# Local attention, then a two-matrix MLP: where the second batch's keys and queries are loaded and turned

## The chip, the cores and the metric

The kernel runs on one core of one Trainium2 chip. The metric is the device time of one execution in microseconds, the median of several runs; less is better. Engines are named as in the profile: PE (TensorE), PEld (its weight loads), DVE (VectorE), ACT (ScalarE), POOL (GpSimd) and SP (SyncE, here only an issuer of DMAs).

## The reference

Batch B = 8, heads H = 8, sequence S = 576, head width D = 64, 8 global positions. Cut to what matters:

```python
mask = np.abs(pos[:, None] - pos[None, :]) <= 32 | is_global[:, None] | is_global[None, :]
scores = np.where(mask, (q @ k.T) / 8, -1e9)
attn = softmax(scores)                       # with 1e-9 added to the sum
x = (attn @ v).transpose(0, 2, 1, 3).reshape(4608, 512)
h = x @ w_in                                 # 512 x 2048
g = h + sin(alpha * h) ** 2 / (alpha + 1e-9)
out = g @ w_out                              # 2048 x 512, float32
```

All inputs are float32 in HBM. The kernel computes in bfloat16, so every load from HBM through POOL's queue is a cast as well.

## The kernel before

The order of the work is written out by hand. For each batch b there are three pieces: `attention(b)`, `gemm1(b)` (x times w_in, and the snake function) and `gemm2(b)` (times w_out). Attention of batch b + 1 and gemm2 of batch b run interleaved on PE: `fill(n)` puts n matrix products of gemm2 between pieces of attention. The program therefore reads attention(0), gemm1(0), attention(1) with gemm2(0), gemm1(1), attention(2) with gemm2(1), and so on.

**gemm1.** It works through 16 blocks `nt` of 128 columns of w_in. For a block PE makes 8 matrix products (`chunks`, L1161) into one of three PSUM buffers (zn, zr, zd in turn); ACT takes the sine into `sb` (L1194); the square goes to ACT (L1197) or to DVE (L1199), as the table `ON_ACT_FIRST` says; DVE multiplies and adds into row nt of `H2` (L1200), which frees the PSUM buffer for block nt + 3.

**The first batches.** Keys and queries have to reach SBUF with the head width on the partitions. Batch 0's are loaded lying (tokens on the partitions) into rows 2 to 7 of H2 and turned by PE. Batches 2 and later are cast to DRAM by POOL (`cast_qk`: kd, qd) and turned by transposing DMAs on SP (`turn_qk`: kt, qt), then copied into place on DVE (`place`, L369). Batch 1's are also loaded lying: `load_lying` (L713) issues four loads into the upper halves of KD and VD, which attention(0) uses until its end, `turn_lying` (L729) turns a third of them on PE with 96 small products into the two PSUM buffers zo, and `place_lying` copies them out: keys on DVE (L737) into KX, queries on ACT (L743) into QX. The three thirds are turned behind blocks 7, 9 and 11 of gemm1(0); the keys are copied ahead of blocks 8, 10 and 12, the queries ahead of blocks 9, 11 and 13. zo is also used by `turn_kq` at block 4, which turns the global keys and queries (L769).

**V.** Batch 0's V is loaded by 16 small DMAs into VD. For batch 1 and later `cast_v` (L343) casts V to DRAM on POOL's queue (vd), and `load_v` (L418) loads it on SP's queue in four DMAs into VX (VD for even batches); `load_vg` (L422) adds the global rows, from VGb, which POOL casts (L761) from what `gather(v, gv)` brought. The numerators of attention (L1009, into zn) read VX; the first of them stand behind the third pair of heads' first scores.

**The queues.** All DMAs that cast are issued by POOL, in program order, on one queue: w_in in four quarters (L430), w_out in four quarters (L436), lying loads, vd, kd, qd. SP's queue has the gathers, the stores of the results (L1261, from osb), the logarithms kept for a later check (LC, L815), VX, MASKT and the transposes.

Of the kernel before, what the change touches and what calls it, by code (L numbers as in the profile page):

```python
# [12 lines left out]
DT = mybir.dt  # L13
# [5 lines left out]
NG = 8  # L19
KT = 48  # L20
# [229 lines left out]
def kernel(  # L250
# [11 lines left out]
    nc = tc.nc  # L262
    B, H, S, D = q.shape
# [3 lines left out]
    NT12 = S // KT  # L267
    NT6 = NT12 // 2
    NK = KT + NG
    NHP = H // 2  # L270
# [121 lines left out]
    def load_v0(hps):  # L392
        for hp in hps:
            for t in range(2):
                for y in range(2):
                    r = t * D + y * 24
                    nc.gpsimd.dma_start(
                        out=VD[r : r + 24, hp, :, t * D : t * D + D],
                        in_=v[0, 2 * hp + t].rearrange("(i a y) d -> y a i d", a=24, y=2)[y],
                    )  # L400

    def load_vg0():
        for h in range(H):
            t = h % 2
            nc.sync.dma_start(
                out=VD[t * D + KT : t * D + NK, h // 2, :, t * D : t * D + D],
                in_=VG0[h::H][:, None, :].to_broadcast([NG, NT12, D]),
            )
# [18 lines left out]
    def load_w_in(gs):  # L427
        for g in gs:
            cols = slice(g * DFF // 4, (g + 1) * DFF // 4)
            nc.gpsimd.dma_start(  # L430
                out=w_in[:, :, cols], in_=moe_w_in[:, cols].rearrange("(c p) n -> p c n", p=P)
            )

    def load_w_out():
# [11 lines left out]
    HK = HH * NT12  # L446
    nat = {w: H2[0 : D + HK, 2 + 3 * w : 5 + 3 * w, :].rearrange("p n c -> p (n c)")[:, 0 : KT * D] for w in (0, 1)}
    gq, gk, gv = [
        H2[0 : NG * B, nt, 0 : 2 * H * D].bitcast(DT.float32).rearrange("p (h d) -> p h d", d=D)
        for nt in (13, 14, 15)  # L450
    ]

    banks = mctx.enter_context(tc.tile_pool(name="banks", bufs=1, space=PSUM))
    zn, zd = [banks.tile([P, 2, 512], DT.float32, name=name) for name in ("zn", "zd")]
# [127 lines left out]
    load_v0((1, 2))  # L582
    load_w_in((1,))
    load_v0((3,))
    load_w_in((2, 3))
    load_vg0()
    gather(q, gq)

# [115 lines left out]
    for e, c0 in ((0, 20), (1, 16)):  # L704
        own = M2[:, :, e].rearrange("p t (x c) -> p t x c", x=2)[:, :, :, c0 : c0 + 24]
        nc.vector.tensor_tensor(out=own, in0=own, in1=farv[:, :, e], op=ALU.max)

    lie = [t[:, NHP * NT12 * D :] for t in (kflat, vflat)]

    def load_lying(t):  # L710

        for w, src in ((1, k), (0, q)):
            nc.gpsimd.dma_start(  # L713
                out=lie[t][D * w : D * w + NHP * NT12],
                in_=src[1].rearrange("(hp t) (i r) d -> t hp i (r d)", t=2, r=KT)[t],
            )

    R16 = KT // 3
    lain = [z.bitcast(DT.bfloat16)[:, 0 : R16 * NHP * NT12] for z in (zo[0][:], zo[1][:])]
# [14 lines left out]
    def place_lying(w, third, copy):  # L734
        A = slice(third * R16 // 2, (third + 1) * R16 // 2)
        if w == 1:
            copy(  # L737
                out=KX[1][:, :, :, 0:KT].rearrange("p h i (y a) -> p h i y a", y=2)[:, :, :, :, A],
                in_=lain[1].rearrange("p (a y h i) -> p h i y a", y=2, h=NHP, i=NT12),
            )  # L740
            return
        for y in range(2):
            copy(  # L743
                out=QX[1][:, :, y, PAD : PAD + 6 * SEG].rearrange("p h (m c) -> p h m c", c=SEG)[
                    :, :, :, 4:
                ].rearrange("p h m (e a) -> p h m e a", e=2)[:, :, :, :, A],
                in_=lain[0].rearrange("p (a y h m e) -> p y h m e a", y=2, h=NHP, m=6, e=2)[:, y],
            )
# [388 lines left out]


    ON_ACT = (1, 3, 5, 7, 9, 11, 13)
    ON_ACT_FIRST = (1, 3, 5, 7, 8, 10, 12, 14)  # L1140
    ON_ACT_SECOND = (1, 3, 5, 7, 9, 10, 12, 13)

    def gemm1(b):


        while len(waiting) > 1:
            fill(1)
        xT = xTs[b]
        r0 = (b % 2) * S
        more = b == B - 1  # L1150
        W = SG if more else S
        hr = tc.alloc_tile_pool(name="hr", bufs=1, space=PSUM)
        hs = {}

        def chunks(nt, cs, parts=slice(0, 2)):
            if nt not in hs:
                hs[nt] = (zn, None, zd)[nt % 3] or hr.tile([P, 2, 512], DT.float32, name="zr")
            h = hs[nt]
            for c in cs:
                for h_part, lo, hi in halves(h, W)[parts]:  # L1160
                    nc.tensor.matmul(  # L1161
                        out=h_part, lhsT=w_in[:, c, nt * P : (nt + 1) * P], rhs=xT[:, c, lo:hi],
                        start=(c == 0), stop=(c == CT - 1), skip_group_check=True,
                    )

        on_act = (ON_ACT_FIRST, ON_ACT_SECOND, ON_ACT)[min(b, 2)]
        for nt in range(NT):
            if b == 1 and nt in (10, 12):
                for which, t, y in PLACES[nt - 6 : nt - 4]:
                    place(2, which, t, y, nc.vector.tensor_copy)  # L1170
            if b == 0 and 8 <= nt < 14:
                third, late = divmod(nt - 8, 2)
                place_lying(1 - late, third, nc.scalar.copy if late else nc.vector.tensor_copy)
            if b == 0 and nt == 4:
                turn_kq()
            if b == 0 and nt == 10:

                cast_globals_v()
                for part in range(3):
                    place_globals(1, part, nc.gpsimd.tensor_copy)  # L1180
                load_vg(1)
            if nt == 0:

                for n in range(2):
                    chunks(n, range(CT - 1), slice(0, 2 - more))
                for n in range(2 * more):
                    chunks(n, range(CT - 1), slice(1, 2))
            chunks(nt, range(CT - 1, CT) if nt < 2 else range(CT))
            h = columns(hs[nt], W)
            fill((GROUP_LAST if more else PER_GROUP)[nt])  # L1190
            if b == 0 and nt in (7, 9, 11):
                turn_lying((nt - 7) // 2)
            sb = spool.tile([P, SG], DT.bfloat16, name="sb")
            nc.scalar.activation(out=sb[:, 0:W], in_=h, func=AF.Sin, scale=alphaT[:, nt : nt + 1])  # L1194
            s2 = spool.tile([P, SG], DT.bfloat16, name="s2")
            if nt in on_act:
                nc.scalar.activation(out=s2[:, 0:W], in_=sb[:, 0:W], func=AF.Square)  # L1197
            else:
                nc.vector.tensor_tensor(out=s2[:, 0:W], in0=sb[:, 0:W], in1=sb[:, 0:W], op=ALU.mult)  # L1199
            nc.vector.scalar_tensor_tensor(  # L1200
                out=H2[:, nt, r0 : r0 + W], in0=s2[:, 0:W], scalar=recipT[:, nt : nt + 1], in1=h,
                op0=ALU.mult, op1=ALU.add,
            )
        hr.release()
# [103 lines left out]
    def phase_a(b_att, b_moe):  # L1308
        def beside(at):

            if b_moe is None:
                if at == 0:
                    second_half()
                    gather(v, gv)
                if at == NHP - 1:
                    load_lying(0)
                if at == NHP:
                    load_lying(1)
                    cast_v(1)
                    for half in range(2):  # L1320
                        rows = slice(half * D, (half + 1) * D)
                        nc.sync.dma_start(out=MASKT[rows], in_=MASK[rows, half * NT6 : (half + 1) * NT6])
                    load_w_out()
                    load_v(1)
                return
            if at == 2 and b_att == B - 1:
                global_rows(slice(0, B - 1))
            if b_att == 5 and at == 3:
                load_columns()
            if 0 <= at < 2:  # L1330
                square_x(b_moe, at)
            if at == 2 and 1 < b_att and b_att + 2 < B:
                pace(xTs[b_att][0:1, 0, 0:1])
                cast_qk(b_att + 2)
                cast_v(b_att + 2)
            if b_moe == 0 and at == 1:
                turn_qk(2)
            for which, t, y in places_at(b_att, at):
                place(b_att + 1, which, t, y, nc.vector.tensor_copy)

        if b_moe is not None:
            waiting.append(gemm2(b_moe))
        attention(b_att, beside)

    phase_a(0, None)
    for b in range(B):
        if b == 1:
            pace(turned[2][0][0:1, 0:1])
            cast_v(2)
            cast_qk(3)  # L1350
            cast_v(3)
        if 0 < b < B - 1:
            load_v(b + 1)
            load_vg(b + 1)
        if b == B - 1:
            global_rows(slice(b, B))
        gemm1(b)
        if b + 1 < B:
            if b == 0:
                cast_qk(2)  # L1360
            elif b + 2 < B:
                turn_qk(b + 2)
            phase_a(b + 1, b)
# [50 lines left out]
```

## Time and profile before

| what | value |
|---|---|
| median of 3 runs (lowest to highest) | 361.01 us (360.44 to 361.14) |
| the profiled execution, its own time | 360.89 us |
| its span, first to last instruction | 359.1 us |
| mean granted TensorE clock | 0.992 |
| PE busy | 325.6 us (91%) |
| ACT busy | 286.4 us (80%) |
| DVE busy | 274.8 us (77%) |
| POOL busy | 58.9 us (16%) |
| DMA bytes, POOL's queue (q0) and SP's (q1) | 18.52 MB and 22.98 MB |

Busy time is the sum over an engine's instructions in one profiled execution; a line of the timeline gives the start, the duration, the engine and line, what is written and read, and in brackets how long the engine stood idle before and which event ended that. The rows of a DMA issue show when the engine issued it, not when its data landed; "DMA to landing" counts from the start of the issue to the last byte's arrival. In the rows of a stretch, PEclk is the share of TensorE's full clock that was granted, and GB/s what all DMA queues moved.

### The profile page before, as it was taken

Reading aid. Unit: us, or ns where it says so; the run is one execution under the profiler, and the core shown is the slowest. Engines: PE = TensorE matmul, PEld = TensorE weight load, DVE = VectorE, ACT = ScalarE, POOL = GpSimd, SP = SyncE. Lnnn points to the kernel's source line nnn. Section 1 sums busy time; section 2 is a strip of 40 time slices with the busy share of each in tenths; the row PEclk is TensorE's granted clock in tenths of the full one; section 3 lists DMA queues with packets and bytes.
Section 4 is the critical chain, followed back from the end, with each engine's and each line's share of the span. In section 5 each row is a group of like instructions: output and inputs, shape, how many; then the busy total and the mean of one; then the engine's idle time right before and its main releaser. Section 6 shows DMA issues by size and latency. Waiting matters only on the chain.

```text
span 359.1 us, 10959 instructions
## 1 busy us (share of the span) xinstructions
PE 325.6 (91%) x4484; PEld 206.8 (58%) x4484; DVE 274.8 (77%) x536; ACT 286.4 (80%) x428; POOL 58.9 (16%) x85
## 2 busy tenths in 40 slices
PE   2668888999899999999999999899999998999992
PEld 1557655556555765577557655576567655664552
DVE  6876866887979787978798788878887876788620
ACT  7779768987889898988998889688988887887510
POOL 7965410051004000400040004000000000004200
PEclk9999989999999999999999999999999999999998
DMA  7999999669988936695759754993251021002132
GB/s 111 114 142 158 160 222 239 143 107 206 189 147 163 171 71 153 126 187 100 133 112 185 146 103 90 197 144 84 63 112 42 2 62 35 29 0 58 51 87 67
DMA packets 87764, 42.27 MB, mean 118 GB/s; under 512 B 72378, under 2 KB 82362, under 8 KB 87322
## 3 DMA queue, kind: packets, MB, share of 16 engines
q0 software_dynamic: 44944, 18.52, 43.1%
q1 hardware_dynamic: 42762, 22.98, 29.1%
q8 instruction: 37, 0.61, 0.7%
q14 instruction: 21, 0.17, 0.2%
HBM read 41.97 MB, written 20.77 MB: 175 GB/s over the span
## 4 chain that ended last, share of the span: by engine, by line
PE 57%; ACT 14%; DVE 13%; DMA 7%; issue 5%; POOL 2%; DVEq 0%; ACTq 0%; POOLq 0%
PE zo L1247 25%; PE zn L1161 9%; DVE H L1200 6%; PE zr L1161 6%; PE zd L1161 5%; ACT sb L1194 5%; PE ring L971 3%; DMA VD<-in_q_dram 3%; DMA H<-in_q_dram 3%; PE zd L1009 2%; DVE s L1199 2%; ACT L947 2%; ACT E L980 2%; ACT s L1197 2%; PE zn L1009 2%
## 5 line engine op out<-in xcount | busy, mean ns | idle before, releaser
L1247 PE MATMUL zo<-w_out,H 128*128 128x512 bf16 (+1 forms) x576 | 148.8, 377 | 0.2 <-DVE E L981 0.2
L1161 PEld LDWEIGHTS <-w_in 128*128 128x128 bf16 x1024 | 99.5, 98 | 49.2 <-issue 16.4
L1247 PEld LDWEIGHTS <-H 128*128 128x128 bf16 x592 | 52.5, 98 | 44.9 <-issue 0.5
L1161 PE MATMUL zn<-xT,w_in 128*128 128x288 bf16 (+1 forms) x384 | 57.0, 287 | 6.9 <-DVE H L1200 3.6
L1194 ACT ACTIVATE sb<-zn,alphaT 128x576 bf16<-128x576 f32 (+1 forms) x48 | 35.7, 743 | 19.5 <-PE zn L1161 19.3
L1161 PE MATMUL zr<-xT,w_in 128*128 128x288 bf16 x320 | 47.8, 288 | 2.1 <-DVE H L1200 2.1
L980 ACT ACTIVATE E<-ring 128x720 bf16<-128x720 f32 x56 | 43.4, 775 | 7.4 <-PE ring L971 6.6
L1200 DVE SCALAR_TENSOR_TENSOR H<-s,recipT,zn 128x576 bf16<-128x576 bf16 (+1 forms) x48 | 39.5, 822 | 11.6 <-ACT s L1197 8.2
L1161 PE MATMUL zd<-xT,w_in 128*128 128x288 bf16 x320 | 47.2, 292 | 0.4 <-DVE H L1200 0.3
L1197 ACT ACTIVATE s<-sb 128x576 bf16<-128x576 bf16 (+1 forms) x58 | 40.0, 689 | 1.8
L981 DVE TENSOR_TENSOR E<-E,MASKT 128x720 bf16<-128x720 bf16 x56 | 29.6, 529 | 14.4 <-ACT E L980 14.1
L1199 DVE TENSOR_TENSOR s<-sb 128x576 bf16<-128x576 bf16 (+1 forms) x70 | 32.0, 458 | 10.5 <-ACT sb L1194 10.5
L1200 DVE SCALAR_TENSOR_TENSOR H<-s,recipT,zr 128x576 bf16<-128x576 bf16 (+1 forms) x40 | 32.9, 822 | 8.8 <-ACT s L1197 6.8
L1200 DVE SCALAR_TENSOR_TENSOR H<-s,recipT,zd 128x576 bf16<-128x576 bf16 (+1 forms) x40 | 32.9, 822 | 6.1 <-ACT s L1197 3.7
L1194 ACT ACTIVATE sb<-zr,alphaT 128x576 bf16<-128x576 f32 (+1 forms) x40 | 29.6, 741 | 8.1 <-PE zr L1161 8.1
L1194 ACT ACTIVATE sb<-zd,alphaT 128x576 bf16<-128x576 f32 (+1 forms) x40 | 29.5, 738 | 4.6 <-PE zd L1161 4.6
L1252 ACT COPY osb<-zo 128x512 f32<-128x512 f32 (+1 forms) x36 | 20.7, 576 | 13.0 <-PE zo L1247 6.7
L820 ACT ACTIVATE R<-L,shift 128x576 f32<-128x576 f32 x32 | 24.9, 778 | 0.5
L347 POOL COPY seen<-xT 1x1 bf16<-1x1 bf16 x4 | 1.7, 428 | 126.6 <-DVE GN L797 126.6
L1234 POOL COPY H<-H 128x16 bf16 x8 | 5.0, 630 | 103.8 <-DVE H L1200 103.4
L1027 DVE TENSOR_TENSOR xT<-zn,R 128x576 bf16<-128x576 f32 x21 | 15.8, 753 | 0.8 <-ACT R L820 0.6
L343 POOL DMA_DIRECT2D vd<-in_v_dram x7 | 16.4, 2337 | 0.1
(185 smaller groups left out, 373.0 us busy)
## 6 DMA issues: line engine op xcount, KB each, us to landing
vd<-in_v_dram POOLq DMA_DIRECT2D x7, 576.0 KB, 14.0
kd<-in_k_dram POOLq DMA_DIRECT2D x6, 576.0 KB, 7.3
qd<-in_q_dram POOLq DMA_DIRECT2D x6, 576.0 KB, 10.2
VX<-vd SPq DMA_DIRECT2D x16, 168.0 KB
w_in<-in_moe_w_in_dram POOLq DMA_DIRECT2D x4, 512.0 KB, 6.7
w_out<-in_moe_w_out_dram POOLq DMA_DIRECT2D x4, 512.0 KB, 19.0
VD<-vd SPq DMA_DIRECT2D x12, 168.0 KB
out_dram<-osb SPq DMA_DIRECT2D x7, 256.0 KB
```

Of the source, the lines that this page charges most:

```text
L343: nc.gpsimd.dma_start(out=cast[b, "vd"][:], in_=v[b].rearrange("h s d -> s h d"))
L820: nc.scalar.activation(out=R[:], in_=L[:], func=AF.Exp, scale=-1.0, bias=shift[:, 0:1])
L980: nc.scalar.activation(out=Eg, in_=zs[:, :, 0 : G3 * WCOL], func=AF.Exp, scale=scale)
L981: nc.vector.tensor_tensor(out=Eg, in0=Eg, in1=MASKT[:, None, G3 * g : G3 * (g + 1), :].rearrange("p o m c -> p o (m c)").to_broadcast([P, ...
L1027: nc.vector.tensor_tensor(out=xT[:, hp, 0:S].rearrange("p (k m c) -> p k m c", k=4, c=KT), in0=tokens(nd(hp, 0)), in1=Rs[hp][:], op=ALU.mult,)
L1161: nc.tensor.matmul(out=h_part, lhsT=w_in[:, c, nt * P : (nt + 1) * P], rhs=xT[:, c, lo:hi], start=(c == 0), stop=(c == CT - 1), skip_group ...
L1194: nc.scalar.activation(out=sb[:, 0:W], in_=h, func=AF.Sin, scale=alphaT[:, nt : nt + 1])
L1197: nc.scalar.activation(out=s2[:, 0:W], in_=sb[:, 0:W], func=AF.Square)
L1199: nc.vector.tensor_tensor(out=s2[:, 0:W], in0=sb[:, 0:W], in1=sb[:, 0:W], op=ALU.mult)
L1200: nc.vector.scalar_tensor_tensor(out=H2[:, nt, r0 : r0 + W], in0=s2[:, 0:W], scalar=recipT[:, nt : nt + 1], in1=h, op0=ALU.mult, op1=ALU.add,)
L1247: nc.tensor.matmul(out=ops[:, cols], lhsT=H2[:, nt, blk * P : (blk + 1) * P], rhs=w_out[:, nt, cols], start=(nt == 0), stop=(nt == NT - 1) ...
L1252: nc.scalar.copy(out=osb[:, cols], in_=ops[:, cols])
```

## The change

The lying keys and queries of batch 1 no longer go into KD and VD but into rows 8 to 10 and 11 to 13 of H2, which nothing uses before gemm1(0) reaches those blocks. They are therefore issued earlier, directly behind batch 0's V and ahead of the second half of w_in, and w_out follows w_in. The turns stand behind blocks 2, 6 and 9, the copies of keys and queries both ahead of blocks 3, 7 and 10. The gathered global rows move to rows 14 and 15. The global rows of V are cast and placed at block 5 instead of block 10, and the cast of batch 1's V comes behind them on POOL, behind w_out. Its load into VX stands behind gemm1(0).

```diff
     gq, gk, gv = [
-        H2[0 : NG * B, nt, 0 : 2 * H * D].bitcast(DT.float32).rearrange("p (h d) -> p h d", d=D)
-        for nt in (13, 14, 15)
+        H2[r : r + NG * B, nt, 0 : 2 * H * D].bitcast(DT.float32).rearrange("p (h d) -> p h d", d=D)
+        for r, nt in ((0, 14), (0, 15), (D, 14))
     ]
+    lie = [H2[:, n : n + 3, :].rearrange("p n c -> p (n c)")[:, 0 : KT * D] for n in (8, 11)]
...
     load_v0((3,))
+    load_lying(0)
+    load_lying(1)
     load_w_in((2, 3))
+    load_w_out()
     load_vg0()
...
-    lie = [t[:, NHP * NT12 * D :] for t in (kflat, vflat)]
...
-    ON_ACT_FIRST = (1, 3, 5, 7, 8, 10, 12, 14)
+    ON_ACT_FIRST = (1, 3, 5, 7, 9, 11, 13, 14)
...
-            if b == 0 and 8 <= nt < 14:
-                third, late = divmod(nt - 8, 2)
-                place_lying(1 - late, third, nc.scalar.copy if late else nc.vector.tensor_copy)
+            if b == 0 and nt in (3, 7, 10):
+                for w, copy in ((1, nc.vector.tensor_copy), (0, nc.scalar.copy)):
+                    place_lying(w, (3, 7, 10).index(nt), copy)
             if b == 0 and nt == 4:
                 turn_kq()
-            if b == 0 and nt == 10:
+            if b == 0 and nt == 5:
                 cast_globals_v()
                 for part in range(3):
                     place_globals(1, part, nc.gpsimd.tensor_copy)
                 load_vg(1)
+                cast_v(1)
...
-            if b == 0 and nt in (7, 9, 11):
-                turn_lying((nt - 7) // 2)
+            if b == 0 and nt in (2, 6, 9):
+                turn_lying((2, 6, 9).index(nt))
...
                 if at == 0:
                     second_half()
                     gather(v, gv)
-                if at == NHP - 1:
-                    load_lying(0)
                 if at == NHP:
-                    load_lying(1)
-                    cast_v(1)
                     for half in range(2):
...
-                    load_w_out()
-                    load_v(1)
...
         gemm1(b)
         if b + 1 < B:
             if b == 0:
+                load_v(1)
                 cast_qk(2)
```

POOL's instructions from the second half of w_in to the casts of batch 2, before (H_97 is H2, KX_94 and QX_96 are batch 1's keys and queries):

```order
L430 DMA w_in<-in_moe_w_in_dram 128x4x512 x2
L713 DMA KD<-in_k_dram 48x1x3072
L713 DMA KD<-in_q_dram 48x1x3072
L713 DMA VD<-in_k_dram 48x1x3072
L713 DMA VD<-in_q_dram 48x1x3072
L343 DMA vd<-in_v_dram 4608x1x64
L436 DMA w_out<-in_moe_w_out_dram 128x4x512 x4
L761 CAST VGb<-H_97 64x512
L377 COPY KX_94<-kTg 128x48x8
L380 COPY QX_96<-qTg 128x4x7x4 x2
L336 DMA kd<-in_k_dram 32x9216
L336 DMA qd<-in_q_dram 32x9216
```

The same place now:

```order
L458 DMA H_97<-in_k_dram 48x1x3072
L458 DMA H_97<-in_q_dram 48x1x3072
L458 DMA H_97<-in_k_dram 48x1x3072
L458 DMA H_97<-in_q_dram 48x1x3072
L430 DMA w_in<-in_moe_w_in_dram 128x4x512 x2
L436 DMA w_out<-in_moe_w_out_dram 128x4x512 x4
L764 CAST VGb<-H_97 64x512
L377 COPY KX_94<-kTg 128x48x8
L380 COPY QX_96<-qTg 128x4x7x4 x2
L343 DMA vd<-in_v_dram 4608x1x64
L336 DMA kd<-in_k_dram 32x9216
```

The four lying loads have moved ahead of w_in, and V's cast (vd) from ahead of w_out to behind it and behind POOL's own copies; the set of transfers up to qd is the same.

SP's queue behind the logarithms of attention(0), before:

```order
L1322 DMA MASKT<-MASK 64x720 x2
L418 DMA VX_93<-vd 24x7x512 x4
L422 DMA VX_93<-VGb 8x7x512 x2
L1261 DMA out_dram<-osb 128x512
L815 DMA LC<-L 2x576
```

The same place now:

```order
L1322 DMA MASKT<-MASK 64x720 x2
L422 DMA VX_93<-VGb 8x7x512 x2
L418 DMA VX_93<-vd 24x7x512 x4
L1265 DMA out_dram<-osb 128x512
L818 DMA LC<-L 2x576
```

The load of VX has changed places with the global rows; the first store and the logarithms of attention(1) stand behind it as they did.

ACT in gemm1(0) before, from the sine of block 8 (into sb from zd) to that of block 11, with the queries' copies (QX_96 from zo_124):

```order
L1194 ACTIVATE sb<-zd,alphaT 128x576
L1197 ACTIVATE s_953<-sb 128x576
L743 COPY QX_96<-zo_124 128x4x6x2x8 x2
L1194 ACTIVATE sb<-zn,alphaT 128x576
L1194 ACTIVATE sb<-zr,alphaT 128x576
L1197 ACTIVATE s_1053<-sb 128x576
L743 COPY QX_96<-zo_124 128x4x6x2x8 x2
L1194 ACTIVATE sb<-zd,alphaT 128x576
```

And now, from the sine of block 2 to that of block 7:

```order
L1198 ACTIVATE sb<-zd,alphaT 128x576
L746 COPY QX_96<-zo_124 128x4x6x2x8 x2
L1198 ACTIVATE sb<-zn,alphaT 128x576
L1201 ACTIVATE s_872<-sb 128x576
L1198 ACTIVATE sb<-zr,alphaT 128x576
L1198 ACTIVATE sb<-zd,alphaT 128x576
L1201 ACTIVATE s_917<-sb 128x576
L1198 ACTIVATE sb<-zn,alphaT 128x576
L746 COPY QX_96<-zo_124 128x4x6x2x8 x2
L1198 ACTIVATE sb<-zr,alphaT 128x576
```

Before, two blocks lay between one pair of copies and the next, and the next turn stood between them; now there are four blocks between the first two pairs and three between the last two.

More of the change, by code (lines that the diff above doesn't have):

```diff
@@ L448, with load_lying @@
     gq, gk, gv = [
-        H2[0 : NG * B, nt, 0 : 2 * H * D].bitcast(DT.float32).rearrange("p (h d) -> p h d", d=D)
-        for nt in (13, 14, 15)
-    ]
+        H2[r : r + NG * B, nt, 0 : 2 * H * D].bitcast(DT.float32).rearrange("p (h d) -> p h d", d=D)
+        for r, nt in ((0, 14), (0, 15), (D, 14))
+    ]
+    lie = [H2[:, n : n + 3, :].rearrange("p n c -> p (n c)")[:, 0 : KT * D] for n in (8, 11)]
+    def load_lying(t):
+        for w, src in ((1, k), (0, q)):
+            nc.gpsimd.dma_start(
+                out=lie[t][D * w : D * w + NHP * NT12],
+                in_=src[1].rearrange("(hp t) (i r) d -> t hp i (r d)", t=2, r=KT)[t],
+            )
     banks = mctx.enter_context(tc.tile_pool(name="banks", bufs=1, space=PSUM))
@@ L706 @@
         nc.vector.tensor_tensor(out=own, in0=own, in1=farv[:, :, e], op=ALU.max)
-    lie = [t[:, NHP * NT12 * D :] for t in (kflat, vflat)]
[L710 to L716, printed above, removed]
     R16 = KT // 3
```

## The prediction

> **What bounds the kernel now.** I read the rows by stage first: up to the first product of gemm1(0), gemm1(0), attention(1) with gemm2(0), and the rest.
>
> ```profile
> core 0: us, PE busy (x) PEld busy (x) DVE busy (x) ACT busy (x) POOL busy (x), PEclk, DMA share, GB/s
> 32.30:59.00 26.70, 21.75 (x333) 15.75 (x335) 18.66 (x30) 20.12 (x32) 9.26 (x13) 0.94 1.28 192
> 59.00:76.30 17.30, 16.79 (x386) 8.81 (x387) 13.02 (x28) 15.56 (x24) 0.12 (x1) 1.00 0.81 167
> 76.30:359.10 282.80, 269.01 (x3505) 166.66 (x3505) 219.11 (x401) 225.08 (x326) 27.04 (x30) 1.00 0.63 106
> ```
>
> From 59 us on PE is busy 97% and then 95% of the stage, so a microsecond won or lost before is passed on to the end. In gemm1(0) nobody is: PE 81%, ACT 75%, DVE 70%. The change lies there. The chain of waits says what holds that stage up:
>
> ```profile
> 32.66 10.86 DMA VD<-in_q_dram
> 43.56 0.68 PE zo L729 x61
> 46.73 0.85 ACT QX L743 x2
> 47.62 0.59 PE zo L729 x51
> 51.58 0.85 ACT QX L743 x2
> 52.47 0.98 PE zo L729 x48
> ```
>
> The last lying load lands at 43.52 and the first turn follows; the second and third turns each follow a pair of query copies on ACT. ACT's timeline has the price: its idle time ahead of the sines of blocks 8, 10 and 12, which are the ones behind the turns.
>
> ```profile
> 45.37 0.74 ACT L1194 ACTIVATE sb<-zd,alphaT 128x576 bf16<-128x576 f32 x1 [0.80 <-PE zd L1161]
> 50.22 0.74 ACT L1194 ACTIVATE sb<-zr,alphaT 128x576 bf16<-128x576 f32 x1 [2.00 <-PE zr L1161]
> 54.58 0.74 ACT L1194 ACTIVATE sb<-zn,alphaT 128x576 bf16<-128x576 f32 x1 [1.51 <-PE zn L1161]
> 59.41 1.28 ACT L947 ACT_TABLE_LOAD   x1
> ```
>
> That is 0.80 + 2.00 + 1.51 = 4.31 us. The table load for attention(1) follows the last sine without a gap, so what ACT saves, attention(1) starts earlier.
>
> **Step 1: the turns go to blocks 2, 6 and 9.** The products and copies stay the same in number; so does ACT's share of squares (8 blocks). What goes is the ring: copies free zo only after the next block's sine and square, the turn waits for them, and the following block waits behind the turn. With three or four blocks between, zo is free long before the next turn. What stays is the turn itself, 0.98 us of PE (the 48 pairs above), three times. PE has waits at those places to put them in:
>
> ```profile
> 34.28 1.14 PE L1161 MATMUL zd<-xT,w_in 128*128 128x288 bf16 x8
> 36.45 1.14 PE L1161 MATMUL zn<-xT,w_in 128*128 128x288 bf16 x8 [1.03 <-DVE H L1200]
> 41.94 1.14 PE L1161 MATMUL zr<-xT,w_in 128*128 128x288 bf16 x8 [0.66 <-DVE H L1200]
> 57.91 0.38 PE L1247 MATMUL zo<-w_out,H 128*128 128x512 bf16 x1
> 66.45 0.48 PE L1009 MATMUL zn<-E,VX 56*64 56x88 bf16 x28
> ```
>
> The first turn fits the 1.03 us wait ahead of block 3; for the other two I count half of each, 0.5 + 0.5. The step wins 4.31 - 1.0 = 3.3 us (at least 4.31 - 3 x 0.98 = 1.4, if nothing hides them; at most 4.3). Attention(1) starts 3.3 us earlier, its first product with w_out at 54.6, its first numerators at 66.45 - 3.3 = 63.15.
>
> **Step 2: can the lying loads be there at block 2?** Block 2 ends on PE at 34.28 + 1.14 = 35.4.
>
> ```profile
> 3.23 8.99 DMA H<-in_q_dram
> 1.47 0.73 POOL L463 DMA_DIRECT2D H<-in_k_dram  x1 [0.42 <-issue]
> 23.71 1.55 POOL L430 DMA_DIRECT2D w_in<-in_moe_w_in_dram  x2
> 30.18 0.65 POOL L713 DMA_DIRECT2D KD<-in_k_dram  x1 [4.92 <-ACT E L846]
> DMA to landing us min/median/max: 7.2/8.7/10.3
> ```
>
> They are now issued from 23.71, in w_in's place. Four loads of this shape took 12.22 - 1.47 = 10.75 us at the start of the program (batch 0's), and 43.52 - 30.18 = 13.3 us here, behind w_in's last quarter, which landed at 24.5 + 10.3 = 34.8 (the last row). So they land between 34.5 and 37.0; I take 36.0. That is 0.6 us late, inside the 1.03 us wait: nothing. At 37.0 it would cost 0.6.
>
> **Step 3: w_in's second half and w_out.** w_in's two quarters came 3.9 us apart (30.9 and 34.8, same row), so behind 36.0 they land at 39.9 and 43.8. The third is wanted by block 8, whose products start at 44.2 now and hardly later then, the fourth four blocks later: hidden. w_out is 4 x 0.524 MB = 2.1 MB; with POOL's queue almost alone the DMAs moved 202 GB/s (the first row below), so 10.4 us: 43.8 + 10.4 = 54.2, and its first quarter at 46.4. Wanted from 54.6: hidden.
>
> ```profile
> 27.00:31.00 4.00, 3.85 (x70) 3.30 (x67) 2.87 (x9) 3.94 (x8) 0.82 (x2) 1.00 1.23 202
> 47.00:57.00 10.00, 8.26 (x167) 5.97 (x167) 6.58 (x9) 6.42 (x13) 0.00 (x0) 0.83 1.20 231
> 265.50:269.00 3.50, 3.50 (x26) 2.35 (x25) 2.71 (x7) 2.61 (x5) 0.00 (x0) 1.00 0.81 187
> ```
>
> **Step 4: V of batch 1, now last.** This is where the change pays.
>
> ```profile
> 33.24 2.25 POOL L343 DMA_DIRECT2D vd<-in_v_dram  x1
> 43.58 0.60 POOL L761 CAST VGb<-H 64x512 bf16<-64x512 f32 x1 [1.88 <-DMA LC<-L]
> 45.59 0.54 POOL L336 DMA_DIRECT2D kd<-in_k_dram  x1
> 47.29 1.83 SPq L418 DMA_DIRECT2D VX<-vd  x4
> 264.41 1.64 SPq L418 DMA_DIRECT2D VX<-vd  x4
> 65.28 0.38 SPq L1261 DMA_DIRECT2D out_dram<-osb  x1
> 67.11 2.41 SPq L353 DMA_TRANSPOSE kt<-kd  x1
> ```
>
> POOL's cast of the global rows waits for the gathers (43.58), with its copies it is done at 45.59, and V's cast is issued there, ready about 47.9. Its turn on the queue comes only when w_out is through, at 54.2, so the late issue is hidden by 6 us. The cast took 47.29 - 43.52 = 3.8 us behind the lying loads; it lands at 58.0. SP then issues the four loads of VX. Alone on the queues they take from 264.41 to about 269 (four times 168 KB, 0.69 MB, against 187 GB/s x 3.5 us = 0.65 MB), 4.5 us: 62.5. But kd and qd of batch 2 (2 x 0.59 MB) run on POOL's queue at the same time: 1.87 MB at 231 GB/s, the rate with both queues at work, is 8.1 us, to 66.1, if VX came last of all. Between 62.5 and 66.1 I take 64.5, a little past the middle since SP's loads neither wait for all of the casts nor run alone. The numerators are ready at 63.15, so PE stands 1.35 us. The scores behind them are queued on PE behind the numerators, and so are fill's products: nothing covers it.
>
> The row is the bound of this step. The Trainium skill, "DMA: Bandwidth & Descriptors", section "Queues, rings and completion order", says that each DMA engine takes turns between the queues that have work, a packet at a time. At half of 231 GB/s VX would need 6.0 us and land at 64.0, with a stall of 0.85 instead of 1.35 (358.5 in the sum below); no run here separates the shares of the two queues yet.
>
> SP waits at the VX load from about 51 to 58; behind it stand the first store (65.28 - 3.3 = 62.0) and the transposes of kt (63.8), neither due before 59.8, so nothing waits for that. kd and qd have the same transfers ahead of them as before. The cast of V costs DVE nothing in gemm1(0) that I can see. One place stays open:
>
> ```profile
> 73.06 0.91 DVE L369 COPY KD<-kt 64x1152 bf16<-64x1152 bf16 x2
> 77.02 2.41 DVE L369 COPY KD<-kt 64x1152 bf16<-64x1152 bf16 x2
> 76.42 2.23 POOL L343 DMA_DIRECT2D vd<-in_v_dram  x1
> ```
>
> The second pair took 1.5 us longer than the first, while POOL issued a cast of V. Both move with attention(1), but not by the same amount: 1.5 us may go or come. I count nothing and keep it for the range.
>
> **Sum.** 360.89 - 3.3 + 1.35 = 358.9 for the profiled execution (span 359.1); the median lies 0.1 above it, so 359.0.
>
> **The rivals.**
> - *V comes late (slower).* The stall replaces the ring. It decides at the point where VX lands at 66.45, when the numerators start now; each microsecond behind that is one lost. For it: another cast of V took much longer than 3.8 us, at best 9.4 from issue to landing:
>
> ```profile
> DMA to landing us min/median/max: 9.4/14.0/23.1
> ```
>
>   The 9.4 is the one at 76.42, alone on its queue, 7.2 us behind its issue's end. With 7.2 for 3.8 the cast lands at 61.4, and with the casts alongside (8.1) VX at 69.5: 3.0 us later than now, 364.0. Against it: in the present order this cast did take 3.8, with little on SP's queue then as now. Chance 0.27.
> - *V is in time.* VX alone on the queues from 58 lands at 62.5, ahead of 63.15: the whole 3.3 us stand, 357.7 on the median's scale. Chance 0.20.
> - *It comes out even.* VX lands within 0.7 us of 66.45, or a stall shorter than that halves PE's clock:
>
> ```profile
> 46.50:49.90 3.40, 1.84 (x72) 1.47 (x70) 2.36 (x4) 1.72 (x4) 0.13 (x1) 0.99 1.23 224
> 49.90:53.30 3.40, 3.21 (x74) 2.02 (x71) 1.61 (x3) 2.81 (x5) 0.00 (x0) 0.51 1.21 230
> ```
>
>   After 3.4 us in which PE was busy 54%, the granted clock was 0.51 for the next 3.4. A stall of 1.6 us makes such a stretch in attention(1), where PE is the bound; half speed over 3.4 us costs 1.7, and 359.0 + 1.7 + 0.25 for the longer stall is 360.95, as before. Chance 0.15. By the Trainium skill, "TensorE: Matmul & The Clock Gate", Part 1, the clock falls after an idle window of about 3.4 us, and a stall of 1.6 would not do it, which would leave 359.3; the rows show that a half idle stretch sufficed here, and the measurement decides.
> - The forecast has the rest, 0.38, with 358 to 360.2 as its own range.
>
> **How the numbers follow.** A run of three rounds tells about 0.2% from no change, 0.72 us. Faster by more: forecast and V in time, 0.58. Within: 0.15. Slower: 0.27. The range runs from V in time with a little of the 1.5 us at DVE (357.7 - 0.5 = 357.2) to 1.8 above now, more than half way to the late case's 364.0: 362.8.
>
> **What would show it.** Right: the lying turns start by 36.5, ACT's idle time ahead of the blocks behind the turns is about 1 us in all, the table load stands near 56.1, SP's VX loads near 58, and PE shows a wait for DMA VX of 1 to 2 us at the first numerators. Wrong: a first turn later than 37.5 (step 2), VX loads issued after 60 (step 4), or a stall over 3.3 us, which eats everything.

## The result, and the profile after

| | before | after |
|---|---|---|
| median, us | 360.80 (22 runs) | 362.01 (359.61 to 365.13, 22 runs) |
| ratio after to before | | 1.0042 [1.0024, 1.0060] |
| the profiled execution, us | 360.89 | 362.83 |
| its span, us | 359.1 | 361.1 |

The change makes the kernel slower by 0.4%; the forecast was 359.0, faster. The ratios and their intervals leave out disturbed runs, such as one of 818.42 us before; the medians are over all runs. The executions after spread over 5.5 us, those before otherwise over 2.0, and the profiled one after stands 0.8 us above its median, so the account below is that of one execution.

To see where the time went, cut both spans at ACT's table loads, which open gemm1(0), attention(1), gemm1(1) and the next attention. These are the rows of busy time by stretch before (PE, PEld, DVE, ACT, POOL, then PEclk, DMA share and GB/s):

```profile
32.84:59.41 26.57, 21.64 (x342) 15.64 (x340) 18.84 (x28) 19.99 (x31) 8.72 (x12) 0.94 1.31 197
59.41:75.65 16.24, 16.07 (x359) 8.31 (x361) 12.41 (x27) 14.52 (x22) 0.00 (x0) 1.00 0.81 166
75.65:98.72 23.07, 20.79 (x187) 14.49 (x176) 19.63 (x30) 18.62 (x28) 5.65 (x5) 1.00 1.36 164
98.72:359.10 260.38, 248.52 (x3348) 152.37 (x3345) 199.68 (x372) 207.10 (x299) 21.50 (x25) 1.00 0.56 101
```

And after:

```profile
33.49:57.14 23.65, 20.48 (x344) 14.99 (x343) 18.42 (x28) 19.91 (x31) 6.98 (x9) 1.00 1.45 205
57.14:78.91 21.77, 16.58 (x353) 8.84 (x359) 12.80 (x27) 14.74 (x23) 4.86 (x5) 0.92 0.93 160
78.91:100.70 21.79, 20.27 (x184) 14.48 (x176) 18.27 (x30) 18.61 (x27) 0.84 (x1) 1.00 1.39 183
100.70:361.10 260.40, 242.59 (x3298) 152.52 (x3345) 199.63 (x372) 207.14 (x299) 21.29 (x25) 1.00 0.55 99
```

The second figure of a row is the stage's length. gemm1(0) won 2.92 us, attention(1) lost 5.53, gemm1(1) won 1.28, the stretch ahead of them lost 0.65, and the 260 us behind did not change: +2.0, the difference of the spans. The 0.65 belongs to this execution rather than to the change: the runs below that share its order of work up to there open gemm1(0) between 32.5 and 33.8 us. What has to be explained lies in attention(1). PE's timeline there, after:

```profile
66.07 0.23 PE L1012 MATMUL zn<-E,VX 56*64 56x88 bf16 x2 [1.95 <-DMA VX<-vd]
68.23 0.49 PE L1012 MATMUL zn<-E,VX 56*64 56x88 bf16 x26 [1.94 <-DMA VX<-vd]
68.66 1.89 PE L1251 MATMUL zo<-w_out,H 128*128 128x512 bf16 x4
```

The brackets say that PE stood idle 1.95 + 1.94 = 3.9 us for the load of VX. The third row is what came on top: four products with w_out in 1.89 us. The rows by stretch give the reason, the granted clock (third figure from the end):

```profile
60.00:62.00 2.00, 2.00 (x23) 0.82 (x21) 1.53 (x2) 1.52 (x3) 0.00 (x0) 1.00 0.76 176
62.00:64.00 2.00, 1.84 (x61) 1.11 (x60) 1.06 (x3) 2.00 (x4) 0.00 (x0) 1.00 0.55 109
64.00:66.00 2.00, 0.12 (x12) 0.00 (x0) 1.92 (x6) 1.88 (x4) 0.00 (x0) 1.00 0.95 186
66.00:68.20 2.20, 0.23 (x2) 0.11 (x2) 0.52 (x2) 0.00 (x0) 0.00 (x0) 1.00 1.25 165
68.20:71.60 3.40, 3.35 (x72) 1.92 (x74) 0.89 (x2) 0.54 (x1) 0.00 (x0) 0.57 1.27 190
```

For 3.4 us behind the wait the clock was 0.57, which costs 0.43 x 3.4 = 1.5 us. Wait and clock make 5.4 of the 5.53.

Why was VX late? SP's timeline shows when its load was issued, and the chain of waits what it waited for:

```profile
57.64 5.37 SPq L418 DMA_DIRECT2D VX<-vd  x4
```

```profile
25.80 11.08 DMA H<-in_k_dram
47.78 9.84 DMA vd<-in_v_dram
60.70 6.64 DMA VX<-vd
```

V's cast landed at 47.78 + 9.84 = 57.6, and the load was issued at once, but the four issues took 5.37 us (1.83 before), the load of the last row landed at 60.70 + 6.64 = 67.3, and the numerators went on at 68.2, 10.6 us behind the first issue. What the two queues moved from 57.6 to 60, from 60 to 62 and from 62 to 64 us, after (packets, MB, and their time as a share of the 16 DMA engines'; q0 is POOL's queue, q1 SP's):

```profile
q0 software_dynamic: 41, 0.48, 94.1%
...
q0 software_dynamic: 22, 0.26, 61.1%
q1 hardware_dynamic: 96, 0.09, 14.4%
...
q1 hardware_dynamic: 225, 0.22, 55.1%
q0 software_dynamic: 9, 0.00, 0.3%
```

In the first stretch SP's queue has no row at all: it had work and moved nothing while the casts of kd and qd ran, 0.09 MB in the second, and came into its own when POOL's queue was empty. Its first packet came 2.8 us behind the issue, and nearly all of VX came behind the casts.

### The profile page after: what moved, and what is told of

Its sections match the earlier page's. It is cut to its first block, busy times and chain, and to the rows that moved or that the text cites. A ratio compares the mean times of both kernels' runs of the same rounds, so it can differ in the third digit from the quotient of the medians.

```text
span 361.1 us, 10896 instructions
## 1 busy us (share of the span) xinstructions
PE 319.4 (88%) x4427; PEld 207.6 (57%) x4484; DVE 273.2 (76%) x536; ACT 286.5 (79%) x428; POOL 59.0 (16%) x85
## 4 chain that ended last, share of the span: by engine, by line
PE 49%; DMA 15%; DVE 12%; ACT 12%; issue 6%; POOL 3%; SPq 1%; DVEq 0%; ACTq 0%; POOLq 0%
PE zo L1251 23%; PE zn L1164 8%; DVE H L1204 6%; PE zr L1164 5%; PE zd L1164 5%; ACT sb L1198 4%; PE ring L974 3%; DMA H<-in_k_dram 3%; DMA vd<-in_v_dram 3%; DMA H<-in_q_dram 3%; PE zd L1012 2%; ACT L950 2%; ACT s L1201 2%; DMA VD<-in_v_dram 2%; DVE s L1203 2%
## 5 line engine op out<-in xcount | busy, mean ns | idle before, releaser
L1251 PE MATMUL zo<-w_out,H 128*128 128x512 bf16 (+1 forms) x519 | 136.1, 378 | 5.7 <-issue 4.9
L1164 PE MATMUL zd<-xT,w_in 128*128 128x288 bf16 x320 | 46.2, 287 | 0.4 <-DVE H L1204 0.3
L974 PEld LDWEIGHTS <-KX 64*64 64x64 bf16 x448 | 8.3, 107 | 14.8 <-issue 14.4
```

Source lines behind the costliest of these rows:

```text
L974: nc.tensor.matmul(out=zs[half * D : (half + 1) * D, t, 0 : G3 * WCOL].rearrange("p (m x c) -> p m x c", x=2, c=60)[:, m % G3, :, c0:c1], ...
L1164: nc.tensor.matmul(out=h_part, lhsT=w_in[:, c, nt * P : (nt + 1) * P], rhs=xT[:, c, lo:hi], start=(c == 0), stop=(c == CT - 1), skip_group ...
L1251: nc.tensor.matmul(out=ops[:, cols], lhsT=H2[:, nt, blk * P : (blk + 1) * P], rhs=w_out[:, nt, cols], start=(nt == 0), stop=(nt == NT - 1) ...
```

## The experiments

Theory A: the place in the order of transfers is what lost. V's load has to wait for casts that are due later. Theory B: the DMA engines have a fixed amount of bytes to move by about 70 us, and whatever stands last in the order is late by as much. Of each expectation the text is that from before the run. A trace is of one execution: those of r2, r3, r5 and r6 took 2.0 to 2.9 us more than the medians of their kernels, so the waits shown for them need not stand in the median execution.

**r1: the changed kernel again**, one profile.

> The changed kernel once more, for the spread of its stall. Both theories: four VX loads issued at about 57.6 us, the first numerators of attention(1) wait for them. Theory A (V's load is held up by what runs beside it) leaves room for another landing, 65 to 68 us; theory B (the last transfer on POOL's queue is late by the amount of bytes ahead of it) gives the same landing within 0.5 us of 67 to 68.

363.14 us, issue of VX 5.35 us, waits for VX of 0.20 and 2.33 us, the last ending at 68.55: the landing repeats, which both theories allow. In gemm1(0), though, this execution took 24.99 us instead of 23.65. PE's timeline and a row by stretch of r1 show where:

```profile
40.36 0.86 PE L772 MATMUL zo<-idf,H 64*128 64x64 f32 x8 [1.77 <-DVE KX L740]
```

```profile
41.00:45.00 4.00, 4.00 (x24) 2.69 (x23) 2.05 (x5) 1.38 (x2) 0.00 (x0) 0.64 1.24 201
```

At block 4 `turn_kq` needs the PSUM buffer that still holds the first turn's keys; PE stood 1.77 us (1.12 in the first profile, at the same line, with the clock at 1.00 behind it) and the clock then fell to 0.64 for about 4 us.

**r2: V's cast ahead of w_out.**

```diff
+    cast_v(1)
     load_w_out()
...
                 load_vg(1)
-                cast_v(1)
```

> V's cast goes back ahead of w_out; all else as changed. Theory A (the change loses by V's load alone): V lands by 55 us, no wait at the first numerators, gemm1(0) keeps its 2.9 us, time 358.0. Theory B (whatever stands last is late): w_out's last quarter lands at about 61 us as in the kernel before, PE wants it at 59, waits 2 us there: about 360.

359.07 us, ratio to before 0.9962 [0.9946, 0.9978]: with this one line back in its old place the change is a gain. The rows of SP and of PE that matter:

```profile
47.76 1.70 SPq L418 DMA_DIRECT2D VX<-vd  x4
```

```profile
61.42 0.81 PE L1251 MATMUL zo<-w_out,H 128*128 128x512 bf16 x3 [1.92 <-DMA w_out<-in_moe_w_out_dram]
```

No numerator waits for VX. Instead w_out's last quarter is 1.92 us late, since VX now ran beside it (from 52 to 58 us SP's queue moved 0.49 MB and POOL's 0.87). This execution took 361.07 us, 2.0 above the median, which may lack that wait. So far B is as good as A.

**r3: V's cast between the halves of w_out.**

```diff
-    load_w_out()
+    load_w_out((0, 1))
+    cast_v(1)
+    load_w_out((2, 3))
...
                 load_vg(1)
-                cast_v(1)
```

(The cut leaves out the new argument of `load_w_out`, the quarters to load.)

> V's cast between the second and the third quarter of w_out. Theory A: V lands at about 52 us, its load even at 10 us is there by 62, w_out's last quarter by 59; time 358.0, the best of the orders. Theory B: one of the two waits about 1 us, 359.

359.53 us, ratio 0.9960 [0.9947, 0.9973]. SP's row and PE's:

```profile
53.63 1.62 SPq L418 DMA_DIRECT2D VX<-vd  x4
```

```profile
65.38 0.23 PE L1014 MATMUL zn<-E,VX 56*64 56x88 bf16 x2 [1.84 <-DMA VX<-vd]
67.05 0.78 PE L1014 MATMUL zn<-E,VX 56*64 56x88 bf16 x26 [1.45 <-DMA VX<-vd]
```

Issued 4 us sooner than after, VX still ended only 1.2 us sooner: from 53.6 to 56 us SP's queue moved nothing, from 56 to 57.5 0.02 MB, and POOL's queue 0.59 and 0.39. From 57.5 to 60 us, with the casts of kd and qd on POOL's queue, the rows are:

```profile
q0 software_dynamic: 36, 0.41, 76.8%
q1 hardware_dynamic: 28, 0.03, 3.9%
```

The two queues moved a like number of packets, and POOL's moved 14 times the bytes.

**r4: kd and qd held back until V has landed.**

```diff
                 load_v(1)
+                pace(VX[1][D : D + 1, 0, 0, 0:1])
                 cast_qk(2)
```

> As changed, but POOL issues the casts of batch 2's keys and queries only when the third of V's four loads is there. Theory A in the form that the casts beside it hold V's load up: the four loads are issued in under 2 us instead of 5.4 and land by 62.5, no wait of over 0.5 us at the first numerators; the casts land some 5 us later (about 69), and the copies of batch 2's keys then wait 2 to 3 us, so the time is 360 to 362. Theory B (SP's load is that slow in itself): issue still over 4 us, landing at 66 or later, 363 or more.

363.12 us, ratio 1.0096 [1.0059, 1.0133]. Without the casts beside it, SP's queue moved its first packet 0.9 us behind the issue; its rows for the same three stretches as above, whose middle one answers after's 0.09 MB:

```profile
q1 hardware_dynamic: 308, 0.30, 47.2%
...
q1 hardware_dynamic: 345, 0.33, 83.2%
...
q1 hardware_dynamic: 184, 0.30, 47.9%
```

The load took 5.6 us (from its issue at 57.48 to its first reader at 63.08) instead of 10.6, nothing waited for VX, and attention(1) took 16.23 us, as before's 16.24. So the casts beside it are what held V's load, and the expectation's rival, a load that is slow in itself, is out. But kd, issued at 63.58, landed at 69.8, and in gemm1(1) PE waited 4.09 us for what DVE does behind the copies of kt: the loss came back there.

```profile
77.24 1.38 PE L1164 MATMUL zn<-xT,w_in 128*128 128x288 bf16 x6 [4.09 <-DVE GN L800]
```

That is against A as I had put it, and for B as put at the head of this section.

**r5: V straight into VX**, by 28 small casting DMAs on POOL's queue, without vd and SP's load.

```diff
     load_w_out()
+    load_v_direct(1, 0)
...
-                cast_v(1)
+                load_v_direct(1, 1)
...
-                load_v(1)
                 cast_qk(2)
```

(The cut leaves out the body of `load_v_direct`.)

> The changed kernel, but batch 1's V is cast straight into VX by 28 small DMAs of POOL, half of them behind w_out, half at block 5; no vd and no load by SP for this batch. Theory A (the loss is V's load on SP's queue, 10.7 us beside the casts of kd and qd where it took 5.6 alone): V lands at 58 to 62 and no numerator waits for it, attention(1) takes 16.2 to 17.5 us as in the kernel before (16.24) instead of 21.8, and 356 to 358 us are left. Theory B (a fixed amount of bytes in the queue, whatever stands last is late): 1.28 MB less are moved, so a part of the gain comes too, but the keys of batch 2 land later than 66 and 2 to 4 us are waited in gemm1(1): 359 to 361.

367.28 us, ratio 1.0168 [1.0146, 1.0190]: both theories missed. The price was one I hadn't counted, POOL's issues:

```profile
53.29 4.22 POOL L425 DMA_DIRECT2D VX<-in_v_dram  x7 [2.15 <-DMA w_out<-in_moe_w_out_dram]
59.88 8.49 POOL L425 DMA_DIRECT2D VX<-in_v_dram  x14
```

At 0.6 us each, with waits between the earlier ones, the last was out at 68.4, and from 62 to 68 us the DMA engines moved 40 to 43 GB/s. The first scores of attention(1) waited 2.88 us for POOL's copies of the global queries, which stand behind the earlier issues. It says nothing about A or B.

**r6 and r9: the casts of kd and qd in small pieces**, 256 elements each, the rest as after; r9 is another execution for its trace.

```diff
             dst, flat = cast[b, name][:], src[b].rearrange("h s d -> (h s d)").rearrange("(p f) -> p f", p=P)
+            if b == 2:
+                dst, flat = [t.rearrange("p (x c) -> x p c", c=256) for t in (dst, flat)]
```

> The changed kernel, but the casts of batch 2's keys and queries run in pieces of 1 KB read and 0.5 KB written instead of some 15 KB. Theory P (a DMA engine takes a packet of each queue in turn, so that each 1 KB packet of V stands behind one of 15 KB that takes 1.27 us): V's load lands at 65 to 66.5 instead of 68.2, SP issues its four DMAs in under 3.5 us instead of 5.4, the stall shrinks from 3.9 to under 2 us, attention(1) from 21.8 to 18 to 20; 360 to 361.5 us unless the keys then land past 66. Theory Q (both queues share bytes, whatever the size of a packet): landing 67.5 to 68.7, issue 5 us or more, 361.5 to 363.

> The same kernel as r6, another execution, for the bytes per queue and the wait that the trace of r6 gave no cause for. Theory P: V's load lands by 65 to 66 and no second wait stands at the numerators; about 361. Theory Q: it lands at 68 or later and both waits are there; 363 or more.

r6: 363.40 us, ratio 1.0047 [1.0017, 1.0076]; r9: 365.20. SP's row and PE's, of r9:

```profile
57.11 1.72 SPq L419 DMA_DIRECT2D VX<-vd  x4
```

```profile
64.00 0.23 PE L1013 MATMUL zn<-E,VX 56*64 56x88 bf16 x2 [1.00 <-DMA VX<-vd]
66.68 0.78 PE L1013 MATMUL zn<-E,VX 56*64 56x88 bf16 x26 [2.46 <-DMA VX<-vd]
```

The long issue (5.37 us) did come from the large packets: it is 1.72 here, and 1.62 in r6. The delay of the start did not: SP's queue moved nothing before 60 us again, while POOL's moved 0.39 MB in each of the two stretches from 56 to 60. VX came 1.5 us sooner and the time didn't fall: attention(1) took 25.6 us in r9, at a mean clock of 0.87 and with another 2.65 us of PE that the trace gives no releaser for (the last section has more on it). Theory P holds for the issue and fails for the start.

**r7: the kernel before, with V's place alone changed**: its cast behind w_out, its load behind gemm1(0), lying loads and turns as they were.

```diff
                     load_lying(1)
-                    cast_v(1)
...
                     load_w_out()
-                    load_v(1)
+                    cast_v(1)
...
             if b == 0:
+                load_v(1)
                 cast_qk(2)
```

> The kernel before with one part of the change alone: the cast of batch 1's V behind w_out on POOL's queue, its load behind gemm1(0); lying loads and turns as before. If V's place is what lost (A and B alike): gemm1(0) stays at 26 to 27 us, the numerators of attention(1) wait 2 to 5 us for V, 363 to 366 us. If the loss came from the earlier lying loads or turns: 360.5 to 361.5.

362.97 us, ratio 1.0067 [1.0040, 1.0094]. SP's row and PE's:

```profile
57.56 5.34 SPq L418 DMA_DIRECT2D VX<-vd  x4
```

```profile
68.02 0.49 PE L1009 MATMUL zn<-E,VX 56*64 56x88 bf16 x26 [2.27 <-DMA VX<-vd]
```

V's place alone costs 0.7%, with the clock at 1.00 all through attention(1). And the numerators start at 68.0, as after (68.2), though attention(1) began 1.2 us later here (58.36 against 57.14): with V last its landing sets the time, and what the turns win in gemm1(0) is only waited for. With before, r2 and after this makes a square:

| ratio to before | V ahead of w_out | V behind w_out |
|---|---|---|
| turns behind blocks 7, 9, 11 | 1 (before) | 1.0067 (r7) |
| turns behind blocks 2, 6, 9 | 0.9962 (r2) | 1.0042 (after) |

V's place makes the difference in both rows; in the right column the intervals of r7 and after overlap, so there the gain of the turns is not clear of noise.

**r8: V's load on POOL's queue**, behind V's cast and ahead of kd and qd.

```diff
-                load_v(1)
+                load_v(1, nc.gpsimd)
                 cast_qk(2)
```

> The changed kernel, but the load of VX for batch 1 goes on POOL's queue, behind the cast of V and ahead of those of kd and qd, instead of on SP's. Theory A, sharpened by the bytes per queue (in the changed kernel SP's queue moved nothing from 57.6 to 60 us and 0.09 MB from 60 to 62, while the casts of kd and qd ran): V now has its turn ahead of the casts and lands at 62 to 63.5, no numerator waits over 0.5 us, and since the queue doesn't run dry between V and kd as in r4 (kd landed at 69.8), the keys land at 65 to 67 and gemm1(1) waits for them under 1.5 us: 356.5 to 359 us. Theory B (a fixed amount of bytes, whatever stands last is late): V's gain is given back by the keys as in r4, a wait of 3 us or more in gemm1(1): 361 to 363.5.

361.29 us, ratio 1.0021 [0.9999, 1.0042], against after's 1.0042. The load was issued at 57.51, each quarter landed 3.5 to 5.0 us behind its own issue and the last at 64.5, a microsecond later than A has it; no numerator waits, since attention(1) began only at 58.75. The keys' transposes were issued at 67.00, inside A's 65 to 67 and without a wait of PE of 1 us or more in gemm1(1). Yet the time is not A's. The profile (span 360.0) names three places: gemm1(0) took 25.76 us, with the wait at `turn_kq` (1.37 us) and the clock at 0.69 behind it as in r1; attention(1) took 17.62, with 1.17 us of PE that the trace gives no releaser for, while kt was being transposed; and the second pair of key copies took 2.45 us again, as before's 2.41.

**r10 and r11: `turn_kq` at block 5**, of r8 and of the changed kernel.

```diff
-            if b == 0 and nt == 4:
+            if b == 0 and nt == 5:
                 turn_kq()
```

> r8 with the turn of the global keys and queries (turn_kq, L772) at block 5 instead of 4. In the profiles of the changed kernel, its repetition and r8, PE stands 1.12, 1.77 and 1.37 us there, since the first turn's keys still lie in the same PSUM buffer, and in two of the three the clock then falls to 0.64 and 0.69 for about four microseconds. Theory C (this wait is the cost of step 1 that was not counted): the wait falls below 0.6, no stretch at half clock follows, gemm1(0) takes 23 to 24 us instead of r8's 25.8, and 359.3 to 360.5 us are left. Rival (the wait only moves, to the second turn behind block 6, or V and the keys take up what is won): 361 to 362.

> The changed kernel with turn_kq at block 5 alone, V's load left on SP. Theory C with V as the bound: gemm1(0) 22.5 to 24 us without a half-clock stretch, but V's load still ends near 68, so the numerators of attention(1) start no earlier and the wait for VX grows by what gemm1(0) wins: 361.5 to 362.5 us. Rival (V's landing isn't what sets the end): 360 to 361.

r10: 361.63 us, ratio 1.0035 [1.0016, 1.0054]; r11: 363.76, ratio 1.0075 [1.0047, 1.0104]. Of PE's timeline in r10:

```profile
39.27 0.86 PE L772 MATMUL zo<-idf,H 64*128 64x64 f32 x8 [0.28 <-DVE KX L740]
...
64.47 0.49 PE L1012 MATMUL zn<-E,VX 56*64 56x88 bf16 x26 [1.84 <-DMA VX<-vd]
...
72.05 0.22 PE L974 MATMUL ring<-QX,KX 64*64 64x88 bf16 x2 [2.70 <-issue]
```

The wait at `turn_kq` shrank to 0.28 (0.79 in r11), the clock stayed at 1.00, and gemm1(0) took 22.8 us in r10 and 22.5 in r11, as theory C has it. Nothing of it reached the end: V's cast still landed at about 57.2, so in r10 PE waited 1.84 us for VX, then 2.70 with no releaser named, beside kt's transposes: the rival's 361 to 362. In r11 the numerators went on at 68.0, as theory C has it, but the time is above either theory's: its first pair of key copies took 3.09 us, from 76.25 on, while POOL issued a cast of V from 76.26 to 79.07, and gemm1(1) took 22.97 instead of after's 21.79.

**r12: the order of need on one queue**: V's cast ahead of w_out (r2) and its load on POOL's queue, so behind w_out and ahead of kd and qd (r8). `turn_kq` stands at block 4.

> One queue in the order of need: the cast of V ahead of w_out (as r2), the load of VX on POOL's queue (as r8), so behind w_out and ahead of kd and qd. In r2 the load of VX (0.69 MB) shared 48 to 54 us with w_out, whose last quarter then landed at 61.4, 1.92 us late, and the clock fell after that; in r8 there was no wait for VX at all. If the order in the queue is what decides (theory A): w_out's last quarter lands 2 to 3 us earlier than in r2, at 58.5 to 59.5, VX at 61.5 to 63.5, no wait over 0.5 us for either, keys as in r2; attention(1) 16.2 to 17.5 us instead of 19.6, and 356.5 to 358.3 us. If the bytes alone decide (theory B): another 1 to 3 us are waited for VX, for the keys, or without a visible cause beside the transposes as in r8 to r10, and it is 358.5 to 360.5, no better than r2.

357.68 us (357.02 to 358.99), ratio 0.9932 [0.9912, 0.9952]: the fastest of all, 0.7% under the kernel before. Its table loads on ACT, and the issues on POOL:

```profile
32.59 1.28 ACT L933 ACT_TABLE_LOAD   x1
56.48 1.28 ACT L951 ACT_TABLE_LOAD   x1
72.70 1.28 ACT L1062 ACT_TABLE_LOAD   x1
95.36 1.28 ACT L951 ACT_TABLE_LOAD   x1
```

```profile
47.52 2.66 POOL L418 DMA_DIRECT2D VX<-vd  x4
50.18 0.57 POOL L336 DMA_DIRECT2D kd<-in_k_dram  x1
```

gemm1(0) takes 23.89 us, attention(1) 16.22, gemm1(1) 22.66; PE waits neither for w_out nor for VX, and kt's transposes are issued at 64.19, sooner than after's 64.84. The DMAs move the same transfers as in after, no later (from 20 to 64 us 8.18 MB, after 7.92), and nothing is late: B falls. What decided is the order. That having it all on one queue added to it is likely, but not clear of noise: r12's interval overlaps r2's, [0.9946, 0.9978].

## Why the prediction was wrong, step by step

**Step 1** held. It gave 3.3 us (1.4 to 4.3); gemm1(0) won 2.92. It had overlooked a wait of its own, the global keys' turn behind the first lying one, 0.2 to 1.8 us of PE in the profiles that have it at block 4 (1.12 after), and a slow clock behind it in three of them (r1, r5, r8). Attention(1) opened 2.27 us earlier and not 3.3: gemm1(0) won 0.4 less, and the stretch ahead lost 0.65.

**Step 2** held: 36.0 for the last lying load, first turn by 36.5; the chain has 25.80 + 11.08 = 36.88, and the bulk of the first turn began at 36.93, 0.4 us past 36.5 and inside the 37.0 of the range.

**Step 3** held in the kernel as changed: no product waited for w_in or w_out.

**Step 4** failed, in one term: the landing of VX, and with it the stall. What came ahead of it was right (V's cast at 58.0; measured 57.6). Then 64.5 was taken, between 62.5 for V alone and 66.1 for V last of all; VX landed at 67.3 and the numerators went on at 68.2. The lower end was about right: r4 has its first reader at 63.1 for V with nothing beside it. Two things were wrong above it. The reason for 64.5, that SP's loads neither wait for all of the casts nor run alone: they wait for nearly all. In after and the five other profiles that issue the load on SP beside the casts of kd and qd (r1, r6, r7, r9, r11) its first packet came 2.8 to 3.6 us behind the issue, where r4 has 0.9. And the price of the upper end, 1.87 MB at 231 GB/s. That rate was read from 47 to 57 us of before, while w_out came; when V's load came into its own after, from 60 to 68.2 us, the last column of the rows above has 176, 109, 186 and 165 GB/s. The stall of 1.35 became 3.9, over the 3.3 that the prediction names as a sign of being wrong. With the numerators ready at its 63.15 the stall would have been 5; they were ready only at 64.1.

The rule of the Trainium skill weighed there ("DMA: Bandwidth & Descriptors", "Queues, rings and completion order", engines take turns between queues a packet at a time) gave 64.0 only with an equal share of the bytes. The runs show no equal share: r3 has 28 packets with 0.03 MB on SP's queue beside 36 with 0.41 on POOL's, whose casts of kd and qd move some 18 KB in a large packet (0.48 MB in 26, with 15 of under 512 bytes, from 57.6 to 60 us after). That is no case against turns by packets. What turns don't give is the late start: nothing from 57.1 to 60 in r9, where POOL's packets are small.

**The clock** was priced, at 1.7 us, but only in the case that comes out even. It can come with a stall near 2 us in other cases too: r2 shows the clock at 0.70 from 61.4 to 65 us behind its 1.92 us. It need not: r7 stood 2.27 us for VX and r10 1.84 and 2.70, with the clock at 1.00 behind them, and what decides is not shown. The page of the Trainium skill on the clock ("TensorE: Matmul & The Clock Gate", Part 1) asks for an idle window of about 3.4 us; in r2 1.9 us without a product, in a stage that had been busy, came ahead of it, so the measurement goes with the prediction's row.

**The copies of kt**, left open at 1.5 us either way, came out as a gain: the second pair took 0.93 us after, instead of 2.41, and gemm1(1) won 1.28. As the prediction suspected, it goes with POOL's casts of V: in all the profiles each pair of 2.4 to 3.1 us runs while POOL issues one, and each pair clear of them takes 0.91 to 0.93. Which pair meets one is a matter of timing (r12's second took 2.37 again), so this gain is luck.

So the sum reads, by the measurement: -2.92 in gemm1(0), +3.9 of waits, +1.5 of clock and 0.1 beside them in attention(1), -1.28 in gemm1(1), +0.65 ahead of them: +2.0. **The rival that came true** is the late V. Its rule, that each microsecond behind 66.45 is lost, holds in r7, where the clock stayed up: the numerators start 1.57 us later than before and the next attention opens 1.55 later. In after 68.2 - 66.45 = 1.8 comes near the 2.0 by luck, since the clock and the gain in gemm1(1) nearly cancel. Its reason was wrong: it had V's cast land late, at 61.4.

## What to carry to other kernels

When an order of transfers is changed, write down for each one its last moment and what has been issued ahead of it on every queue, and price a load that meets earlier casts by what those casts are: beside w_out it moved over a third of the bytes (r2), behind the casts of kd and qd it moved little until they were through (after, r3). Put transfers with close deadlines in the order of need, on one queue if that keeps it (r12: the same bytes, 4.3 us less than after by the medians). And a gain ahead of a fixed landing is worth nothing until the landing moves (r7 and after both start at 68).

## What was not expected of the hardware

- A load on SP's queue moved nothing for 2.4 us from its issue while POOL's queue had casts of kd and qd in flight that had been issued earlier, against 0.30 MB in the same 2.4 us with the casts held back. Its first packet came 2.8 us behind the issue instead of 0.9, and later still (3.6) in r9 with the casts in small packets. What delays the start is not shown.
- Four issues on SP took 5.34 to 5.37 us beside casts with large packets of some 18 KB (after, r1, r7, r11), and 1.6 to 1.8 beside small ones or none.
- In r6, r8, r9 and r10 PE stopped for 1.0 to 2.7 us with no releaser in the trace, each time at the same place of the program, between the 11th and the 12th of the last 14 score products of attention(1). It went on 1.2 to 1.5 us behind the end of a 16 KB packet on the queue called instruction (q8; in r10 the packet lies at 69.86 to 70.82 and PE goes on at 72.05). In the other profiles that packet had ended 1.3 to 4.0 us ahead of the product. So PE probably waited for its own instructions; a run that moves the packet alone is missing, and why it came late stays open. It started while kt or qt was being transposed. The unnamed waits of r6 (4.36 us) and r11 (2.31) stand elsewhere, at the numerators that wait for VX in after. The row of r10 from 69 to 70 us:

```profile
q8 instruction: 1, 0.02, 6.0%
```
